# Heads of one layer in two 40-row halves, gate pieces together and one product for both memories in a two-layer memory transformer

## The chip, the cores and the metric

The kernel runs on one core of a Trainium2 chip. The metric is the device time of one execution in microseconds (us); lower is better. All times below are us unless marked ns. PE is TensorE, DVE is VectorE, ACT is ScalarE, POOL is GpSimd and SP is SyncE, which issues most transfers.

## The reference

Two layers run one after the other over x of 2048 rows and 448 columns (bf16). Each layer is a recurrent memory attention A and a gated feed-forward part B, both behind a layer norm and with the same weights in both layers:

```python
for s in range(n_seg):                          # 64 segments of 32 rows
    h = concatenate([mem, x[:, 32*s : 32*s+32]])  # 8 memory rows + 32 rows
    q, k, v = h @ Wq, h @ Wk, h @ Wv            # 16 heads of 256
    p = softmax(mask(q @ k.T * 256**-0.5))
    o = (p @ v) @ Wo
    mem = o[:, :8]                              # read by the next segment
    outs.append(o[:, 8:])
# A: x = x + outs;   B: x = x + (relu(n @ W_gate) * (n @ W_up)) @ W_down, n = layernorm(x), 1792 hidden
```

The mask lets every row see the 8 memory rows, and a row of the segment see itself and the rows before it. Since a segment needs the memory of the one before, the 64 segments of a layer are a chain.

## The kernel before

**Folding.** Scores are h M h^T with M = Wk Wq^T for each head, and the output is P h B with B = Wv Wo. M and B (tiles M_sb, MT_sb, B_sb, BT_sb) are made once, while the first steps run. The 448 columns are handled as three slices of 128 and a tail of 64; the tail products use half the PE array (64 rows), in pairs.

**Steps.** There are 70 steps, g = 0 to 69. Layer 1 is chain C1, layer 2 is chain C2, which runs 6 steps (LAG) behind. Steps 0 to 5 work on C1 alone and 64 to 69 on C2 alone (function single, L599); steps 6 to 63 work on both (function dual, L803). One step does, in PE's order:

1. G = M h for all heads (tile gps in PSUM, copied to G by ACT and DVE; GPhase.run). The first G products of a step read the memory columns of hTr that the step before wrote last.
2. The mask product that begins the scores' tile S_ps, then the hook mid() with other work.
3. The tails of the memory values and of the scores, then the three main slices of the scores.
4. The softmax on DVE and ACT: reduce (mx), subtract (se), exp, sum, reciprocal, weighting into PW, and a transpose of P in 32x32 blocks on DVE into TW.
5. Beside it, on PE, the values h B (tile vps): VOm of the memory rows and of half a segment, vox of a segment. Class Values does this in parts; ACT and DVE copy each bank (L419). The hooks soft(), before() and late() put other work between them.
6. The output product: AT_ps (rows) or, in steps of one layer that do not end a block, yt and yt3 (function columns, L760, transposed already).
7. The memory rows are turned into columns (mps) and copied into hTr for the next step; the hooks end() and last() follow.

The order of PE's instructions is the order in which the code records them (in_order); DVE, ACT and POOL are ordered by the tile scheduler. PSUM is one pool of eight banks.

**In a step of one layer** the scores stand in two tiles SX and SM of 160 columns, four groups of 32 rows each, the tails wait once on POOL for a token (pass_on, fence), and TW comes from two DVE transposes (L665).

**The feed-forward part** works on blocks of 128 rows, when four segments of a chain are done. It is cut into ten pieces: turn, seven gate_up of 28 products each (PSUM tiles gate and up, copied by ACT to ut and by DVE to hh), and two downs of seven products each (dps; the second adds into x_ring at L358). They wait in ffn_q, one queue for each chain, and fill(chain, n) takes n of them. Which hook takes how many depends on g % 4. Steps with g % 4 == 1 read:

```python
def mid():
    prep_rows(C1, gb + 2, recent["G"])
    fill(0, 2)                      # two gate_up
def before():
    fill(0, 3)                      # one gate_up, two downs
    prep_stats(C2, gb - 1)
    prep_rows(C2, gb - 1)
```

prep_stats and prep_rows make the normalized rows (xn) of the next block: statistics on DVE (L258, L260), the power on POOL (L262, L263), the scaling on DVE (L276). prep_pe in end() turns xn on PE (tps) and copies it to hTr (L298). In single, load_when ties a load of feed-forward weights on SP's queue to certain instructions.

Of the kernel before, what the change touches and what calls it, by code (L numbers as in the profile page):

```python
# [9 lines left out]
BF = mybir.dt.bfloat16  # L10
# [25 lines left out]
RB2 = 64  # L36
NR = 12
# [13 lines left out]
def build_kernel(ctx, tc, A_x, A_mem0, A_Wq, A_Wk, A_Wv, A_Wo, B_W_gate, B_W_up, B_W_down, out,  # L51
# [18 lines left out]
    make_identity(nc, ident[:])  # L70

# [60 lines left out]
    def matmul(*a, **k):  # L132
        op = nc.tensor.matmul(*a, **k)  # L133
        in_order(op)
        if fence:
            sync(op, fence.pop())
# [15 lines left out]
    for q in PWs + [TW]:  # L152
        nc.gpsimd.memset(q[:], 0.0)
# [445 lines left out]
    def single(g, c, inG, mid, soft, before, late, end, last):  # L599
# [7 lines left out]
        mT = memTp[g % 2]  # L607
        SX, SM = [psum.tile([P, 512], F32, tag="ps", name="S_ps") for _ in HALVES]
        N = 4 * L
        matmul(SX[:, 0:N], selq[LO], maskb[LO, 0:4], start=True, stop=False, skip_group_check=True)  # L610
# [3 lines left out]
        vm = Values(lambda rr, k: mT[rr, k, :], VOm, [cp_a, cp_a, cp_a, cp_a])  # L614
        cols = hT[:, :, cid, 0:SEG], mT

        def tails(m, k, e):
            half = HALVES[e]
            ps = (SX, SM)[m][32 * k:32 * k + 32, 0:N].rearrange("p (s e t) -> p s e t", s=2, e=2)
            matmul(ps[:, :, e, :], cols[m][half, 3, :], G[half, :, 7 * k + 3, cid, :], start=(m == 1 and e == 1),  # L620
                   stop=False, tile_position=(half.start, 32 * k), skip_group_check=True)

        for e in range(2):
            for k in range(4):
                tails(0, k, e)
                tails(1, k, 1 - e)
            if not e:
                passed = pass_on()
                if g:
                    vm.both(True)  # L630
                fence.append(passed)
        for m, ps in enumerate((SX, SM)):
            for sl in range(3):
                for k in range(4):
                    t = 7 * k + sl
                    matmul(ps[32 * k:32 * k + 32, 0:N], cols[m][:, sl, :], G[:, :, t:t + 5:4, cid, :], start=False,
                           stop=(sl == 2), tile_position=(0, 32 * k), skip_group_check=True)

        mx = p_soft.tile([P, H], F32, tag="mx", name="mx")
# [3 lines left out]
        for m, ps in enumerate((SX, SM)):  # L643
            q = slice(4 * m, 4 * m + 4)
            S3 = ps[:, 0:N].rearrange("p (h k) -> p h k", k=L)
            nc.vector.tensor_reduce(mx[:, q], S3, axis=AX.X, op=ALU.max)
            nc.vector.tensor_tensor(se[:, q], S3, mx[:, q].unsqueeze(2).to_broadcast([P, 4, L]), op=ALU.subtract)
            vm.after = nc.scalar.activation(se[:, q], se[:, q], AF.Exp, scale=SCALE)
            load_when(vm.after)
        nc.vector.tensor_reduce(ssum[:, 0:8], se[:, 0:8], axis=AX.X, op=ALU.add)  # L650
        nc.vector.reciprocal(rs[:, 0:8], ssum[:, 0:8])
        PW = PWs[g % 2]
        odd = g % 2

        def weigh(kind, slots, keys):

            dst = PW[:, 8 * kind:8 * kind + 8].rearrange("p (g m) t -> p m g t", m=2)
            n = keys.stop - keys.start
            nc.vector.tensor_tensor(dst[:, :, :, slots], se[:, 0:8, keys].rearrange("p (m g) t -> p m g t", m=2),
                                    rs[:, 0:8].rearrange("p (m g) -> p m g", m=2).unsqueeze(3).to_broadcast([P, 2, 4, n]),  # L660
                                    op=ALU.mult)

        def turn_P(kind):
            b = slice(8 * kind, 8 * kind + 8)
            load_when(nc.vector.transpose(TW[:, b, :].rearrange("p b t -> p (b t)"),  # L665
                                          PW[:, b, :].rearrange("p b t -> p (b t)")))

        if odd:
            weigh(1, slice(0, 16 + MEM), slice(16, L))
            turn_P(1)  # L670
            weigh(0, slice(0, 16), slice(0, 16))
        else:
            weigh(1, slice(16, 16 + MEM), slice(SEG, L))
            turn_P(1)
            weigh(0, slice(0, SEG), slice(0, SEG))
        turn_P(0)
# [26 lines left out]
        if v is not None:  # L703
            v.bank(1 - odd, 0)
            v.bank(1 - odd, 1)
        late()

        flat = TW[:, :, :].rearrange("p b t -> p (b t)")
        order = [(1, 0), (1, 1), (1, 2), (1, 3), (0, 0), (0, 1), (0, 2), (0, 3)]
        nxt = g + 1 - c.lag < nseg  # L710
        if nxt and not ends:
            columns(g, c, flat, (vox, VOm), order)
            end()
            last()
            return
        at = [psum.tile([P, 512], F32, tag="ps", name="AT_ps") for _ in HALVES]
        cols = (slice(0, 256), slice(256, DM))
        for kind, gs in order:
            src = (vox, VOm)[kind]
            side, e = divmod(gs, 2)  # L720
            o = 64 * (4 * kind + gs)
            for half, ps, cc in zip(HALVES, at, cols):
                matmul(ps[half, 0:cc.stop - cc.start], flat[:, o:o + 64], src[:, 2 * e + side, cc],
                       start=((kind, gs) == order[0]), stop=((kind, gs) == order[-1]), tile_position=(0, half.start),
                       skip_group_check=True)
# [7 lines left out]
        if nxt:  # L733
            tps = [psum.tile([P, 2, MEM], F32, tag="ps", name="mps") for _ in HALVES]
            m = slice(SEG, L)
            for kd in range(2):
                for half, ps in zip(HALVES, tps):
                    for lo in ((0,) if kd == 0 or half is LO else (0, 64)):
                        w = mb[half, 128 * kd:128 * kd + (64 if kd and half is HI else 128)]
                        o = ps[lo:lo + 64, kd] if kd and half is HI else ps[:, kd]  # L740
                        matmul(o, w, ident[half, half.start + SEG + 16:half.start + L + 16], start=True, stop=True,
                               skip_group_check=True)
            r = (g + 1) % NR
            cp_v(hTr[:, r, 0:2, cid, SEG:L], tps[0][:])
            op = cp_a(hTr[:, r, 2:4, cid, SEG:L], tps[1][:])
            if ut is not None:
                behind(ut, op)
            columns_of(g + 1, [c])
# [11 lines left out]
    def columns(g, c, flat, src, order):  # L760

        yt, yt3 = [psum.tile([P, 512], F32, tag="ps", name=n) for n in ("yt", "yt3")]
        W = L + 16

        def mains(some):
            for kind, gs in some:
                side, e = divmod(gs, 2)
                o = 64 * (4 * kind + gs)
                for sl in range(3):
                    matmul(yt[:, sl * W:sl * W + W], src[kind][:, 2 * e + side, 128 * sl:128 * sl + 128],  # L770
                           flat[:, o:o + W], start=((kind, gs) == order[0] and not sl),
                           stop=((kind, gs) == order[-1]), skip_group_check=True)

        mains(order[:6])
        for kind, gs in order:
            side, e = divmod(gs, 2)
            o = 64 * (4 * kind + gs)
            for half in HALVES:
                matmul(yt3[half, 0:W], src[kind][:, 2 * e + side, 384:DM], flat[:, o:o + W],
                       start=((kind, gs) == order[0]), stop=((kind, gs) == order[-1]), tile_position=(0, half.start),  # L780
                       skip_group_check=True)
        mains(order[6:])
        hT = hTr[:, (g + 1) % NR, :, c.cid]
        ym = yt[:, 0:3 * W].rearrange("p (k t) -> p k t", t=W)
        cp_v(hT[:, 3, SEG:L], yt3[:, W - MEM:W])
        cp_v(hT[:, 0:3, SEG:L], ym[:, :, W - MEM:W])
# [16 lines left out]
    def dual(g, chains, inG, mid, soft, before, late, end, last):  # L803
# [141 lines left out]
        if nxt:  # L945
            tps = {c.cid: psum.tile([P, NSL, MEM], F32, tag="ps", name="mps") for c in nxt}
            for kd in (2, 3, 1, 0):
                for c in nxt:
                    half = HALVES[c.cid]
                    m = c.rb + SEG  # L950
                    matmul(tps[c.cid][:, kd], mb[half, 128 * kd:128 * kd + 128], ident[half, m:m + MEM],
                           start=True, stop=True, skip_group_check=True)
            for c in nxt:
                eng = cp_v if c is C1 and not ends else cp_a
                op = eng(hTr[:, (g + 1) % NR, :, c.cid, SEG:L], tps[c.cid][:])
                if ut is not None and eng == cp_a:
                    behind(ut, op)
            columns_of(g + 1, nxt)
# [66 lines left out]
    for g in range(nsteps):  # L1025
# [25 lines left out]
        elif r == 1:  # L1051
# [3 lines left out]
            def mid():  # L1055
                prep_rows(C1, gb + 2, recent["G"])
                fill(0, 2)

            def before():
                fill(0, 3)  # L1060
                prep_stats(C2, gb - 1)
                prep_rows(C2, gb - 1)

# [98 lines left out]
```

## Time and profile before

| what | value |
|---|---|
| median of 9 runs | 1517.39 us |
| lowest and highest | 1514.95 and 1519.29 us |
| profiled execution: its time | 1515.34 us |
| profiled execution: span | 1513.5 us |
| PE busy, share of the span | 1484.7 us, 98% |
| DVE, ACT, POOL busy | 958.9, 600.8, 150.5 us |
| steps of both layers, by g % 4 = 0, 1, 2, 3 | 21.75, 24.32, 20.95, 19.25 us |
| steps 0 to 5 | 35.42, 13.59, 13.04, 14.48, 15.04, 18.55 us |
| steps 64 to 69 | 16.56, 20.45, 15.73, 15.36, 12.23, 27.53 us |

The length of a step is taken from its first G product to that of the next step. Step 0's length holds the start of the kernel's main part, and step 69's the last feed-forward block. In the lines of a timeline the columns are start, length, engine, line, operation, output<-input, tile size, shape and count. A product's "length" in such a line includes a pipeline of some 150 to 250 ns, so the distance of starts, not the length, is what it costs PE. In the chain the columns are start, length, what. In the list of waits they are what waited, for whom, in total, how often and the longest.

### The profile page before, as it was taken

What the parts mean: (1) busy time and instruction counts of PE and PEld (TensorE: products, weight loads), DVE (VectorE), ACT (ScalarE), POOL (GpSimd) and SP (SyncE); (2) the same over time, 40 slices, a digit from 0 to 9 for tenths busy, and PEclk for the clock granted to TensorE, in tenths of its full rate; (3) what the DMA queues carried; (4) which work ended last, traced back from release to release, by engine and by line L of the source; (5) the groups of instructions that cost most, each with busy time, mean ns of one, the idle gap of its engine ahead of it and who ended that gap; (6) DMA issues with size and microseconds to landing.
All of it is one profiled execution on the core that took longest, in us unless ns stands there. A gap on an engine that the chain in (4) does not pass through costs nothing.

```text
span 1513.5 us, 89312 instructions
## 1 busy us (share of the span) xinstructions
PE 1484.7 (98%) x41984; PEld 1139.6 (75%) x41984; DVE 958.9 (63%) x2236; ACT 600.8 (40%) x1410; POOL 150.5 (10%) x534
## 2 busy tenths in 40 slices
PE   7999999999999999999999999999999999999998
PEld 4567777778777777877778777877778777877786
DVE  6635566666666566666666666666666665666544
ACT  5644333433344343434343343434334343434343
POOL 1001011010101001010100101010001100011000
PEclk9999999999999999999999999999999999999999
DMA  9731001010000100010000000000000000000000
GB/s 234 175 95 41 5 13 15 12 20 13 14 14 15 18 12 20 12 22 13 8 19 14 20 12 20 12 21 7 15 18 13 17 12 15 13 6 14 5 8 9
DMA packets 82801, 39.40 MB, mean 26 GB/s; under 512 B 65176, under 2 KB 81536, under 8 KB 82432
## 3 DMA queue, kind: packets, MB, share of 16 engines
q1 hardware_dynamic: 82400, 33.68, 10.1%
q8 instruction: 328, 5.37, 1.4%
q14 instruction: 41, 0.34, 0.1%
q10 hardware_dynamic: 32, 0.01, 0.0%
HBM read 14.00 MB, written 1.84 MB: 10 GB/s over the span
## 4 chain that ended last, share of the span: by engine, by line
PE 95%; DMA 2%; DVE 2%; SPq 1%; ACT 1%; issue 1%; POOL 0%; POOLq 0%; ACTq 0%
PE gps L133 31%; PE vps L133 29%; PE gate L133 9%; PE S_ps L133 6%; PE AT_ps L133 6%; PE dps L133 6%; PE up L133 3%; PE ps L133 2%; DMA xnT<-xd 1%; PE yt L133 1%; SPq L175 1%; PE mps L133 0%; DMA wq<-in_A_Wq_dram 0%; PE tp L145 0%; DMA wvn<-in_A_Wv_dram 0%
## 5 line engine op out<-in xcount | busy, mean ns | idle before, releaser
L133 PE MATMUL gps<-hTr,M_sb 128*128 128x80 bf16 (+1 forms) x11760 | 413.6, 198 | 2.4 <-issue 2.4
L133 PEld LDWEIGHTS <-M_sb 128*128 128x128 bf16 x11760 | 403.9, 99 | 7.0 <-issue 2.8
L495 DVE CAST G<-gps 128x480 bf16<-128x480 f32 (+4 forms) x327 | 194.7, 611 | 217.4 <-PE gps L133 217.0
L495 ACT CAST G<-gps 128x480 bf16<-128x480 f32 (+4 forms) x327 | 165.6, 525 | 340.4 <-PE gps L133 340.4
L133 PEld LDWEIGHTS <-hTr 128*32 128x32 bf16 (+1 forms) x8512 | 174.7, 95 | 161.4 <-issue 44.9
L133 PE MATMUL vps<-B_sb,hTr 128*32 128x448 bf16 x4464 | 234.2, 353 | 0.0
L133 PE MATMUL gate<-xnT,Wgu 64*128 64x128 bf16 x3136 | 204.5, 217 | 1.8 <-ACT xnT L333 1.0
L133 PE MATMUL up<-xnT,Wgu 64*128 64x128 bf16 x3136 | 204.7, 217 | 0.5 <-issue 0.5
L133 PEld LDWEIGHTS <-Wgu 64*128 64x128 bf16 x6272 | 186.0, 94 | 21.3 <-issue 19.3
L133 PEld LDWEIGHTS <-memTp 128*32 128x32 bf16 (+1 forms) x5880 | 136.9, 95 | 64.8 <-issue 2.4
L133 PE MATMUL vps<-B_sb,memTp 128*32 128x448 bf16 x3360 | 171.7, 353 | 0.2 <-issue 0.2
L419 ACT CAST vox<-vps 128x448 bf16<-128x448 f32 x186 | 96.1, 533 | 186.2 <-PE vps L133 186.2
L346 DVE SCALAR_TENSOR_TENSOR hh<-gate,ut 128x256 bf16<-128x256 f32 x224 | 93.6, 418 | 66.5 <-ACT ut L345 66.3
L419 ACT CAST VOm<-vps 128x448 bf16<-128x448 f32 x251 | 120.7, 526 | 1.5 <-PE vps L133 1.4
L345 ACT CAST ut<-up 128x256 bf16<-128x256 f32 x224 | 83.8, 374 | 73.1 <-PE up L133 72.4
L419 DVE CAST vox<-vps 128x448 bf16<-128x448 f32 x186 | 104.7, 599 | 5.6 <-PE vps L133 5.4
L133 PEld LDWEIGHTS <-TW 128*32 128x32 bf16 (+1 forms) x3760 | 93.1, 97 | 13.4 <-DVE TW L665 1.9
L862 ACT ACTIVATE se<-se 128x320 f32<-128x320 f32 x116 | 54.5, 470 | 117.2 <-DVE se L861 117.2
L133 PE MATMUL gps<-hTr,MT_sb 64*128 64x80 bf16 (+1 forms) x3920 | 91.5, 195 | 2.9 <-ACT MT_sb L197 0.7
L133 PE MATMUL dps<-Wd,hh 128*128 128x448 bf16 x448 | 92.7, 354 | 0.0
L892 DVE STREAM_TRANSPOSE TW<-PW 128x512 bf16<-128x512 bf16 x116 | 75.3, 685 | 21.1 <-POOL PW L874 21.1
L133 PEld LDWEIGHTS <-MT_sb 64*128 64x128 bf16 x3920 | 76.3, 96 | 14.1 <-DVE mv L260 4.8
(110 smaller groups left out, 1411.4 us busy)
## 6 DMA issues: line engine op xcount, KB each, us to landing
wo<-in_A_Wo_dram SPq DMA_DIRECT2D x8, 448.0 KB, 5.6
wvn<-in_A_Wv_dram SPq DMA_DIRECT2D x8, 384.0 KB, 3.9
y<-mb SPq DMA_DIRECT2D x87, 28.0 KB, 1.8
out_dram<-x_ring SPq DMA_DIRECT2D x16, 112.0 KB, 1.7
Wgu<-in_B_W_gate_dram SPq DMA_DIRECT2D x7, 224.0 KB, 3.3
Wgu<-in_B_W_up_dram SPq DMA_DIRECT2D x7, 224.0 KB, 3.3
Wd<-in_B_W_down_dram SPq DMA_DIRECT2D x7, 224.0 KB, 2.7
x_ring<-in_A_x_dram SPq DMA_DIRECT2D x10, 112.0 KB, 2.9
```

Source lines behind the costliest of these rows:

```text
L133: op = nc.tensor.matmul(*a, **k)
L175: in_order(nc.sync.dma_start_transpose(t[:], srcs[n][:, 1024 * i:1024 * (i + 1)]))
L345: recent["ut"] = nc.scalar.copy(ut[:], gu[1][:])
L346: recent["hh"] = nc.vector.scalar_tensor_tensor(out=self.hh[:, f:f + 2, :], in0=gu[0][:], scalar=0.0, in1=ut[:], op0=ALU.max, op1=ALU.mult)
L419: op = self.evac[2 * x + e](self.dst[:, 2 * e + x, :], self.ps[x][e][:, 0:DM])
L495: op = (cp_a, cp_v)[self.side](gp.G[:, self.side, self.t0:self.t0 + self.n, gp.c0:gp.c1, :], self.ps[:, 0:self.n * gp.NP].rearrange("p (m ...
L862: vm.after = nc.scalar.activation(se[:, q], se[:, q], AF.Exp, scale=SCALE)
L892: load_when(nc.vector.transpose(TW[:, b, :].rearrange("p b t -> p (b t)"), PW[:, b, :].rearrange("p b t -> p (b t)")))
```

## The change

The change has four parts.

- In single, the scores of a step stand in one tile of 320 columns: eight heads in rows 0 to 39, eight in rows 64 to 103 (sel, PARTS). The token on POOL goes. The softmax runs once over 104 rows. P is transposed by four PE transposes into PT_ps, two copied by ACT, two by DVE, between the two value banks. Columns are 40 wide in place of 56.
- In steps with g % 4 == 1, mid() takes three gate_up and before() the two downs.
- In step 5 (g + 1 == LAG), what was before() becomes soft(), so the downs and the statistics and rows of C2 come ahead of the memory values' mains.
- In dual, with g % 4 == 1 and both chains going on, the two memories are turned by four products over 128 rows and one ACT copy, in place of eight over 64 rows and two copies.

```diff
+PARTS = (slice(0, SEG), slice(SEG, L))
+    sel = glob.tile([P, P], BF)
+    for half in HALVES:
+        nc.vector.tensor_tensor(sel[:, half], ident[:, LO], ident[:, HI], op=ALU.add)
...
+    PT = p_pp.tile([P, 4, P], BF, name="PT")
...
     def single(...)
-        SX, SM = [psum.tile([P, 512], F32, tag="ps", name="S_ps") for _ in HALVES]
-        N = 4 * L
-        matmul(SX[:, 0:N], selq[LO], maskb[LO, 0:4], start=True, stop=False, skip_group_check=True)
+        S = psum.tile([P, 512], F32, tag="ps", name="S_ps")
+        N = 8 * L
+        matmul(S[:, 0:N], sel[LO, :], maskb[LO], start=True, stop=False, skip_group_check=True)
         mid()
...
-        for e in range(2):
-            for k in range(4):
-                tails(0, k, e)
-                tails(1, k, 1 - e)
-            if not e:
-                passed = pass_on()
-                if g:
-                    vm.both(True)
-                fence.append(passed)
...
+        def S_tail(e, stop):
+            half = HALVES[e]
+            for q in PARTS:
+                r = 64 * e + q.start
+                matmul(S[r:r + q.stop - q.start, 0:N], hT[half, 3, cid, q], G[half, :, 3:NGH:7, cid, :], start=False,
+                       stop=stop, tile_position=(half.start, r), skip_group_check=True)
+
+        if g:
+            for e in range(2):
+                vm.part(e, True)
+                S_tail(e, False)
...
+        for sl in range(3):
+            for e in range(2):
+                for q in PARTS:
+                    r = 64 * e + q.start
+                    matmul(S[r:r + q.stop - q.start, 0:N], hT[:, sl, cid, q], G[:, :, sl + 4 * e:sl + 4 * e + 22:7, cid, :],
+                           start=False, stop=(g > 0 and sl == 2), tile_position=(0, r), skip_group_check=True)
...
+        nc.vector.tensor_reduce(mx[R2, 0], S3, axis=AX.X, op=ALU.max)
+        nc.vector.tensor_tensor(se[R2, 0:8], S3, mx[R2, 0].unsqueeze(2).to_broadcast([n, 8, L]), op=ALU.subtract)
+        vm.after = nc.scalar.activation(se[R2, 0:8], se[R2, 0:8], AF.Exp, scale=SCALE)
...
-        def turn_P(kind):
-            b = slice(8 * kind, 8 * kind + 8)
-            load_when(nc.vector.transpose(TW[:, b, :].rearrange("p b t -> p (b t)"),
-                                          PW[:, b, :].rearrange("p b t -> p (b t)")))
...
         before()
         if v is not None:
             v.bank(1 - odd, 0)
+        for q, Pt, cp in ((0, Px, cp_a), (2, Pm, cp_v)):
+            PT_ps = psum.tile([P, 4, P], BF, tag="ps", name="PT_ps")
+            for x in range(2):
+                transpose(PT_ps[:, x, R2], Pt[R2, 4 * x:4 * x + 4, :], ident[R2, R2])
+            load_when(cp(PT[:, q:q + 2, R2], PT_ps[:, 0:2, R2]))
+        late()
+        if v is not None:
             v.bank(1 - odd, 1)
-        late()
...
     def dual(...)
         if nxt:
...
+            if len(nxt) == 2 and g % 4 == 1:
+                tps = psum.tile([P, NSL, 2, MEM], F32, tag="ps", name="mps")
+                pick = ident[:, :].rearrange("p (c t) -> p c t", c=2)[:, :, SEG:L]
+                for kd in (2, 3, 1, 0):
+                    matmul(tps[:, kd], mb[:, 128 * kd:128 * kd + 128], pick, start=True, stop=True,
+                           skip_group_check=True)
+                cp_a(hTr[:, (g + 1) % NR, :, :, SEG:L], tps[:])
+            else:
...
         elif r == 1:
             def mid():
                 prep_rows(C1, gb + 2, recent["G"])
+                fill(0, 3)
+
+            def before():
                 fill(0, 2)
-
-            def before():
-                fill(0, 3)
                 prep_stats(C2, gb - 1)
                 prep_rows(C2, gb - 1)
+
+            if g + 1 == LAG:
+                soft, before = before, none
```

## The prediction

> **What bounds the kernel now.** I read the page first (busy shares, then the chain that ended last), then PE's list of waits, then single stretches as timelines and chains: one dual step with g % 4 == 1 (step 21, 474.67 to 498.99), one step of C2 alone (66), the last step of C1 alone (5) and an early one (2).
>
> ```profile
> span 1513.5 us, 89312 instructions
> PE 1484.7 (98%) x41984; PEld 1139.6 (75%) x41984; DVE 958.9 (63%) x2236; ACT 600.8 (40%) x1410; POOL 150.5 (10%) x534
> PE 95%; DMA 2%; DVE 2%; SPq 1%; ACT 1%; issue 1%; POOL 0%; POOLq 0%; ACTq 0%
> ```
>
> PE is the chain (95%), at a granted clock of 0.999. So time can be won or lost in two ways only: PE's own starts (how many products, how far apart, how many changes of array shape), and the rare waits of PE. Those waits are few:
>
> ```profile
> PE tps L145 <- DVE xn L276: 3.0, 3, 1.7
> PE gps L133 <- issue: 2.4, 4, 1.2
> PE AT_ps L133 <- DVE TW L665: 1.1, 1, 1.1
> PE S_ps L133 <- POOL token L140: 0.2, 1, 0.2
> ```
>
> The profiled run took 1515.34 with a span of 1513.5; the median of the nine runs, 1517.39, is 2.05 above it. I sum differences against the profiled run and put them on the median. 0.2% is 3.0 us, about what a measurement of this kernel can tell from no change.
>
> **Part 1: dual steps with g % 4 == 1 and both memories going on (9, 13, ... 61: 14 of them).** Step lengths from first G product to first G product: 24.32 for nearly all. The timeline of step 21, PE's rows:
>
> ```profile
> 488.78 0.57 PE L133 MATMUL vps<-BT_sb,hTr 64*32 64x448 bf16 x16
> ...
> 490.18 2.82 PE L133 MATMUL dps<-Wd,hh 128*128 128x448 bf16 x14
> ...
> 497.05 0.39 PE L145 MATMUL tps<-ident,xn 128*128 128x128 bf16 x4
> 497.37 0.26 PE L133 MATMUL mps<-ident,mb 64*128 64x8 bf16 x8
> 497.55 1.50 PE L133 MATMUL dps<-Wd,hh 128*128 128x448 bf16 x7
> ```
>
> Between the value tails (64x32 tiles) and the downs lies the third gate piece, 28 products of 64x128. From the last tail's start, 489.009 in the single records, to the first down is 1.169. Without the piece one change of shape remains: tail to another shape takes 0.281. In mid() the piece follows two others of the same shape, which run at 27.75 ns a start (56 in 1.79 with one change): 28 x 27.75 = 0.777. So 1.169 - 0.281 - 0.777 = 0.111 saved per step, which is one drain: in the same records the change from tails to gate costs 281 where 187 is usual, and gate to downs 148 where 56 is.
>
> The memories' turn: from the last tps start (497.216) to the next down (497.554) is 0.338, of which 0.151 is the change to 64x128, then eight products at about 24 ns. After: no change of shape, 56 ns for the last tps, then four 128x128 loads with 16 columns. The trace has none of 16 columns; the nearest row is G's 128x128 products with 40 columns, 25 to 28 ns a start. 56 + 4 x 27 = 0.164, so 0.174 saved. Bounds: if starts were only as dense as the transposes (56 ns) 0.06 would be saved; at 24 ns a start 0.186.
>
> Sum 0.285 x 14 = **-4.0** (bounds -2.4 to -4.3). What has to hide: the third hh is done before the softmax's first reduce; the transposed P comes 0.78 later, near 491.6, against AT's start at 494; the third hh, which the downs read, comes before them and not beside them. One ACT copy instead of two lies under the 1.43 of the last downs. The tight cover is DVE's:
>
> ```profile
> 497.76 0.63 DVE L258 BATCH_NORM_STATS2 stats<-x_ring 128x6 f32<-128x448 bf16 x1
> 498.42 0.29 DVE L298 COPY hTr<-tps 128x256 bf16<-128x256 bf16 x1
> ```
>
> C2's new columns are in hTr at 498.71; the next G starts at 498.99. After, DVE's chain hangs on AT, which moves by 0.111 (to 498.60), and G moves by 0.285 (to 498.70). The margin is 0.1; if it is gone, up to 0.1 to 0.18 a step is lost.
>
> **Part 2: the 12 steps of one layer (0 to 5, 64 to 69).** S becomes one tile of 320 columns in two 40-row halves. Its mask product streams 320 columns, not 160: +0.07. Mains: 12 products of 320 in groups of four, instead of 24 of 160: 0.54 against 0.47, which is in the yt times below. The tails no longer need POOL's token, and need fewer G copies at once. Early steps waited there; the chain in step 2:
>
> ```profile
> 69.66 0.21 PE S_ps L133 x8
> ...
> 69.92 0.11 POOL token L140
> ...
> 70.07 0.58 PE S_ps L133 x20
> ```
>
> Tails and mains took 1.24, 1.17 and 1.02 in steps 1 to 3 and 0.90 in 68, against 0.70 where nothing waits: I take 0.33, 0.45, 0.33 and 0.2 off, -1.3 in all.
>
> Against that stand four transposes on PE in place of two on DVE. In step 66 the old ones cost PE nothing:
>
> ```profile
> 1449.89 0.76 DVE L665 STREAM_TRANSPOSE TW<-PW 128x256 bf16<-128x256 bf16 x2
> ...
> 1451.02 1.32 PE L133 MATMUL vps<-B_sb,hTr 128*32 128x448 bf16 x24
> ...
> 1452.27 0.48 PE L133 MATMUL yt<-TW,VOm 128*128 128x56 bf16 x12
> ```
>
> TW is whole at 1450.65, while PE wants it at 1452.27. The four transposes go between the two value banks: one change of shape in (0.105), three starts at 56 (0.168), one out (0.151): 0.42, whether or not anything waits. S mains start at 1446.41. The new softmax (one reduce 0.49, one subtract 0.49, exp 0.47, sum 0.48, reciprocal 0.2, two weighings 0.5) is ready some 3.6 after the first S main; PE comes at 3.8. The copies are new waits: DVE's copy of P's transpose stands behind its vox copy (0.6), and with it yt starts 4.83 after the first S main instead of 4.36. I take 0.47 a step (bounds 0.22, four starts of 56 ns, and 1.0, if exp queues behind a VOm copy of 0.51 on ACT). Steps 0 to 4, 64 and 66 to 68: 9 x 0.47 = +4.2, nine mask products +0.6, waits -1.3: **+3.5**. Narrower columns (40, not 56) save nothing: both start every 27 ns. In 69 PE waited 1.1 for TW, and the new path through PE and a copy is about as long: 0. In 65 a chain of x_ring, statistics, rstd, xn sets the end as before: 0. load_when's weights move one issue later on SP's queue, long before their use: 0. Setup: two DVE adds and a POOL memset while PE waits for the first weights: 0.
>
> The Trainium skill speaks against this part: "TensorE: Matmul & The Clock Gate", Part 4: PE-mode transpose, gives about 275 ns to a transpose in a kernel and asks for a copy out of PSUM. By that figure four would be an estimated 1.1 us, and the twelve steps about 9 us dearer than my sum. This trace's transposes last 219 ns each but start every 56 ns, so I hold to the starts; the copy is in the sum.
>
> **Part 3: step 5.** Its downs now run ahead of the memory values' mains. Before:
>
> ```profile
> 152.78 0.64 DVE x_ring L358
> ...
> 155.28 0.41 DVE xn L276
> ...
> 155.74 0.46 PE tps L145 x4
> ...
> 156.56 0.96 PE gps L133 x37
> ```
>
> PE stood 1.9 before the second tps. Downs that end near 150.3 put this chain's end near 153.4. But DVE's order has P's transposed copy behind xn: it comes at 153.45, yt starts at 153.75 and not 153.1, and takes 1.1; tps follow at 154.85, and the two hTr copies let G start at about 156.05: **-0.5** (0 if DVE is later still; -1.9 if the copy does not hold yt).
>
> **Pauses of PE that nothing explains.** The 2.4 under issue and some smaller gaps lie a multiple of 128 products apart in the steps of one layer, some 0.5 each, 5 us in all; the regular spacing suggests the loading of instructions, which the page lists as a queue of its own, but no row proves it. About 300 products fewer is two such places fewer of some 28: -0.3 (bounds -1.5 and +1, since all places shift).
>
> **Sum:** -4.0 + 3.5 - 0.5 - 0.3 = **-1.3**: 1514.0 for the profiled run, 1516.1 on the median. Its own range, 1514.2 to 1518.1.
>
> **Rivals.**
> *A, the steps of one layer cost less.* The old steps also change shape before yt, so the transposes may cost only their four starts (0.22): -2.2 in nine steps; step 5 gets its whole 1.9: -1.4. For it: DVE and ACT are less busy in these steps. Against: DVE's order in step 5. All of it is -4.9; with most of it -4.5, 1512.9.
> *B, slower: P's transpose becomes a wait.* Place: the copy of P's transpose on DVE in the nine steps. The softmax now starts only when all of S is done, exp stands behind the first VOm copy on ACT's queue, and with the PE margin of 0.2 gone, the second value bank is late as well. Price 1.0 instead of 0.47: -1.3 + 9 x 0.53 = +3.5, 1520.9. It decides from 0.95 a step. For it: the thin margin. Against: in step 66 that VOm copy (1447.88, 0.51) would end 1.9 after the first S main, so exp, wanted at 1.7, is held by 0.2 alone.
> *C, the saving of part 1 does not reach the next G*, since DVE's copy of hTr ends last: 14 x 0.18 given back, +1.2, 1518.6.
>
> **How the numbers follow.** My sum 0.40 (0.06 of it beyond -3.0), A 0.36, B 0.17, C 0.07. Faster: 0.36 + 0.06 = 0.42; within: 0.34 + 0.07 = 0.41; slower: 0.17. The range runs from past A's -4.9 to most of B, 1511.8 to 1520.5: about 1 in 10 is left out on each side.
>
> **What would show it.** Steps 9 to 61 with g % 4 == 1 at 24.03 instead of 24.32, gate pieces in one run, four mps of 128x16. Steps 64, 66 and 67 longer by about 0.5, with PT_ps near 3.8 after S. Step 5 at about 18.0. The other dual steps unchanged at 21.75, 20.95 and 19.25. I am wrong if PE waits for PT in the steps of one layer by over 0.3, if hTr releases G after the steps of part 1, or if steps that the diff does not touch change.

## The result and the profile after

The changed kernel takes 1510.16 us (median of 10 runs, 1508.47 to 1512.63) beside 1517.12 of the kernel before (32 runs, 1513.36 to 1521.28). The ratio is 0.9954 with a 95% interval of 0.9944 to 0.9963: 7.0 us faster. The forecast was -1.3, and the time lies below its range, 1511.8 to 1520.5. Its profiled run took 1511.46, of which the span is 1509.7.

The page of the changed kernel, the lines that answer to those of before:

```profile
span 1509.7 us, 88653 instructions
PE 1484.4 (98%) x41688; PEld 1136.0 (75%) x41688; DVE 953.2 (63%) x2202; ACT 603.0 (40%) x1396; POOL 149.9 (10%) x523
PE 95%; DMA 1%; DVE 1%; SPq 1%; ACT 1%; issue 0%; POOL 0%; POOLq 0%; ACTq 0%
```

PE is still the chain, and its busy time is the same within 0.3 us: this sum can't show where 7 us went. PE's list of waits:

```profile
PE gps L138 <- issue: 1.7, 4, 0.7
PE yt L138 <- DVE PT L701: 1.2, 1, 1.2
PE AT_ps L138 <- DVE PT L701: 1.1, 2, 0.7
PE tps L150 <- DVE xn L282: 0.6, 1, 0.6
```

The tps waits for xn fell from 3.0 to 0.6, and waits for P's transposed copy (PT) came in their place, in steps 5, 65 and 69. The wait for POOL's token is gone.

**Dual steps.** All 14 with g % 4 == 1 take 0.30 less (most of them 24.32 before and 24.02 after, forecast 24.03); the other dual steps stand at 21.75, 20.95 and 19.25 as before, save for step 6 and for single excursions of up to 0.7 in both profiles. Step 21's PE rows after:

```profile
489.12 0.57 PE L138 MATMUL vps<-BT_sb,hTr 64*32 64x448 bf16 x16
489.62 2.82 PE L138 MATMUL dps<-Wd,hh 128*128 128x448 bf16 x14
...
496.50 0.39 PE L150 MATMUL tps<-ident,xn 128*128 128x128 bf16 x4
496.72 0.25 PE L138 MATMUL mps<-ident,mb 128*128 128x16 bf16 x4
496.82 1.49 PE L138 MATMUL dps<-Wd,hh 128*128 128x448 bf16 x7
```

The downs follow the value tails after 0.50 and not 1.40, since the third gate piece now stands in mid(), and from tps to the next downs it is 0.32, not 0.50. The four products over 128 rows start about 25 ns apart. 14 x 0.30 = 4.2 of the 7.0 are here.

**Steps of one layer.** From the profile before to the one after, steps 0 to 5 become 2.1 shorter in all, step 6 becomes 1.5 longer, steps 64 to 68 become 2.2 longer and step 69 becomes 2.3 shorter. Two things that have nothing to do with the amount of work make up much of these differences: falls of PE's granted clock, and pauses of PE, in which it stands and no row names what it waits for. The clock first. Rows of the view by stretches (length, busy time and count of PE, PEld, DVE, ACT, POOL, then the granted clock, DMA share and GB/s) in the last feed-forward block, before:

```profile
1500.13:1502.00 1.87, 1.87 (x40) 1.87 (x41) 0.00 (x0) 0.35 (x1) 0.00 (x0) 0.57 0.18 58
1502.00:1504.00 2.00, 2.00 (x47) 2.00 (x43) 0.85 (x2) 0.40 (x2) 0.00 (x0) 0.55 0.00 0
1504.00:1507.30 3.30, 3.30 (x122) 3.23 (x116) 1.51 (x4) 1.49 (x4) 0.00 (x0) 1.00 0.02 5
```

and of the changed kernel, the same block and then the beginning of step 6:

```profile
1497.95:1500.00 2.05, 2.05 (x74) 2.05 (x75) 0.42 (x1) 0.64 (x2) 0.00 (x0) 1.00 0.13 45
...
155.98:157.30 1.32, 1.32 (x37) 1.21 (x36) 0.00 (x0) 0.46 (x2) 0.00 (x0) 0.50 0.00 0
157.30:159.00 1.70, 1.70 (x28) 1.70 (x27) 0.00 (x0) 0.29 (x1) 0.00 (x0) 0.50 0.00 0
```

For 3.4 us the clock is half, the same products start every 53 ns and not every 28, and 1.7 us are lost. PE is "busy" all the while, so no busy sum shows it. Each profile has such falls at other places: that of before has one, the block above; that of the changed kernel has two, in the setup (at 33) and in step 6. In the profiles of all the kernels below, 23 falls lie ahead of the program's last product. Each lasts 3.41 us, falls of one run lie a whole multiple of 3.41 us apart (30.0, 36.0, 13.0 and so on), and in the 3.41 us ahead of each PE had stood for 1.3 to 2.3 in all. Stretches of this grid with up to 1.9 of standing had no fall behind them, so the standing time alone does not tell when a fall comes. The mean clock of a run tells how many falls it had. Over 34 runs of the kernel before, beside the first experiments:

| mean clock | runs | mean time |
|---|---|---|
| 1.000 | 2 | 1514.0 |
| 0.999 | 10 | 1515.8 |
| 0.998 | 16 | 1517.3 |
| 0.997 | 6 | 1519.9 |

Their mean is 0.9982; the changed kernel's is 0.9991, and 0.0009 of 1513 us is 1.3 to 1.4 us. (The kernel before had 0.9984 to 0.9987 in the later groups of runs.)

### The profile page after: what moved, and what is told of

It is laid out like the page before. It is cut to its first block, busy times and chain, and to the rows that moved or that the text cites. A ratio compares the mean times of both kernels' runs of the same rounds, so it can differ in the third digit from the quotient of the medians.

```text
span 1509.7 us, 88653 instructions
## 1 busy us (share of the span) xinstructions
PE 1484.4 (98%) x41688; PEld 1136.0 (75%) x41688; DVE 953.2 (63%) x2202; ACT 603.0 (40%) x1396; POOL 149.9 (10%) x523
## 4 chain that ended last, share of the span: by engine, by line
PE 95%; DMA 1%; DVE 1%; SPq 1%; ACT 1%; issue 0%; POOL 0%; POOLq 0%; ACTq 0%
PE gps L138 32%; PE vps L138 29%; PE gate L138 8%; PE AT_ps L138 6%; PE S_ps L138 6%; PE dps L138 5%; PE up L138 4%; PE ps L138 2%; PE yt L138 1%; DMA xnT<-xd 1%; SPq L181 1%; PE mps L138 0%; DMA wq<-in_A_Wq_dram 0%; PE tp L150 0%; DMA wvn<-in_A_Wv_dram 0%
## 5 line engine op out<-in xcount | busy, mean ns | idle before, releaser
L138 PEld LDWEIGHTS <-hTr 128*32 128x32 bf16 (+2 forms) x8464 | 172.4, 95 | 160.2 <-issue 47.6
L138 PE MATMUL gate<-xnT,Wgu 64*128 64x128 bf16 x3136 | 199.8, 216 | 1.4 <-ACT xnT L339 1.0
L138 PE MATMUL up<-xnT,Wgu 64*128 64x128 bf16 x3136 | 200.0, 216 | 0.0
L138 PEld LDWEIGHTS <-memTp 128*32 128x32 bf16 (+1 forms) x5640 | 131.4, 95 | 66.5 <-issue 2.3
L138 PEld LDWEIGHTS <-TW 128*32 128x32 bf16 x3712 | 90.8, 97 | 11.0 <-DVE TW L885 0.7
```

## The experiments

Theory 1 says that products and waits of PE alone set the time, theory 2 that falls of PE's clock after gaps do as well, theory 3 that pauses of PE that come with its number of instructions do. Medians stand beside the runs of the kernel before in the same group of runs (1517.1, 1517.5, 1516.5, 1517.0 and 1516.7).

**1. The kernel before once more** (no edit).

> The kernel before, unchanged, to see its spread and where PE's granted clock falls. Theory 1 (products and waits alone): the ratio is 1, and the runs differ by some 0.5 us around their median, with no pattern in the clock. Theory 2 (clock): PE's granted clock falls to 0.5 for some 3.4 us after stretches in which PE idles, each fall costs about 1.6 us and lowers a run's mean clock by 0.001; so the runs spread over some 5 us, the profile shows one to three falls, and these lie behind the second tps of step 5, the tps waits of steps 65 and 69 or the setup, not always the same. Theory 3 (pauses of PE without a releaser): they stay where they were, at the same products, and are about 5 us again.

1517.61, ratio 1.0003 (0.9993 to 1.0013), mean clock 0.9982. The profile has a fall in step 0 and one in step 6, none in the last block (step 69: 25.62, not 27.53). In step 6, after the 1.89 wait of step 5:

```profile
159.77:161.50 1.73, 1.73 (x57) 1.66 (x57) 0.00 (x0) 0.35 (x1) 0.00 (x0) 0.85 0.03 9
161.50:164.50 3.00, 3.00 (x50) 3.00 (x48) 0.66 (x1) 1.07 (x2) 0.00 (x0) 0.52 0.00 0
```

The places differ from run to run, as theory 2 has it.

**2. The dual part alone.**

```diff
 mid():    fill(0, 2) -> fill(0, 3)      before(): fill(0, 3) -> fill(0, 2)
 dual:     four 128x128 mps products, one ACT copy, for g % 4 == 1
```

> Only the three gate pieces in mid() for g % 4 == 1 and the one product for both memories; heads and step 5 as before. Theory 1: the 14 dual steps with g % 4 == 1 at 24.02 (-0.30 each, -4.2), step 65 0 to -1 by its earlier downs; -4.2 to -5.2 in all, so 1512 to 1513 beside 1517.1. Theory 2: about the same -4.2, and -1 to -2 more if the tps wait of step 65 was a place of clock falls. If the whole gain of 7.0 is here, the heads and step 5 are worth nothing.

1513.29, ratio 0.9975 (0.9966 to 0.9985): -3.8. The 14 steps are at 24.02. Mean clock 0.9983, as before.

**3. The gate pieces alone** (one run).

> The kernel before with three gate pieces in mid() and two downs in before() for g % 4 == 1, and nothing else. Prediction: 24.32 - 0.11 = 24.21 in the 14 dual steps; with the changed kernel's 24.02 the memories' one product then has 0.19 (predicted 0.17). Step 65 shorter by 0.3 to 0.6, since its downs end earlier and its tps no longer wait.

The one run took 1515.13, which alone says nothing. The steps with g % 4 == 1 are at 24.21, to the hundredth what was forecast, so the memories' product has 0.19. Step 65 took 20.22 (20.45 before), less than expected. The profile of step 21:

```profile
492.55 0.57 PE L133 MATMUL vps<-BT_sb,hTr 64*32 64x448 bf16 x16
493.06 2.82 PE L133 MATMUL dps<-Wd,hh 128*128 128x448 bf16 x14
...
500.25 0.26 PE L133 MATMUL mps<-ident,mb 64*128 64x8 bf16 x8
500.43 1.50 PE L133 MATMUL dps<-Wd,hh 128*128 128x448 bf16 x7
```

**4. The heads alone** (single, columns, sel and PT of the changed kernel).

> Only the heads of one layer in two 40-row halves (with the PE transposes, the 40-wide columns, the new setup tiles); steps with g % 4 == 1 and step 5 as before. My prediction: +3.5 -0.3, so about +3.2. Theory 1 with the sizes of the changed kernel's profile: +0.4 in each of steps 4, 64, 66, 67 and about -0.5 in steps 1 to 3, -0.7 in 69: 0 to -1. Theory 2: a further -1 to -2 from fewer falls of the clock. Theory 3: the pauses move to other products, +1 to -2.

1514.81, ratio 0.9985 (0.9977 to 0.9994): -2.3. My +3.2 looked plainly wrong here; experiments 12 to 17 say more.

**5. The swap in step 5 alone.**

```diff
+            if g + 1 == LAG:
+                soft, before = before, none
```

> Only the downs, statistics and rows of step 5 ahead of the memory values' mains (the hooks swapped at g + 1 == LAG). Prediction: without the PE transposes nothing holds yt, so the second tps no longer waits 1.9: -1.0 to -1.9. Theory 1: just that. Theory 2: up to -1.6 more where the clock fell after that wait, in the share of runs in which it did: -2 to -3 in the median.

1515.41, ratio 0.9988 (0.9980 to 0.9997): -1.7. The second tps waits no more, but the downs now wait 0.6 for the last hh, so step 5 itself went from 18.34 (18.55 in the first profile) to 18.14 only. The mean clock rose from 0.9982 to 0.9992, some 1.4 of the 1.7. Most of the gain is the clock.

**6. Useless work in the gaps of the kernel before.**

```diff
+    def warm(n):
+        ps = psum.tile([P, 4, P], BF, tag="ps", name="warm_ps")
+        for i in range(n):
+            transpose(ps[:, i % 4], ident[:], ident[:])
 end():  prep_pe(C1, gb + 2); fill(1, 1)
+        warm(31) in step 5, warm(19) in step 65
         prep_pe(C2, gb - 1)
 turn(): + warm(20) ahead of and warm(20) behind the tps of step 69
```

> The kernel before with useless PE transposes of the identity put into four of its gaps: 31 ahead of the second tps of step 5 (a wait of 1.89), 19 ahead of the tps of step 65 (1.11), 20 ahead of the tps of step 69 and 20 behind them (1.2 each). Theory 1 (only products and waits count): the gaps are filled, nothing becomes faster, 0 to +0.5. Theory 2 (clock): the granted clock no longer falls in step 6 or in the last feed-forward block; the mean clock rises from 0.9982 to about 0.9992, and the median falls by 1.0 to 2.0 although PE has 90 products more.

1514.29, ratio 0.9981 (0.9972 to 0.9989): 90 products more and 3.2 us less. The mean clock is 0.9995, the profile has no fall at all before the end. Theory 1 falls. The gain is more than expected: the kernel before stood at 0.9985 in this group, so the clock accounts for some 1.4 of it, and the rest is open.

**7. Useless work in step 5 alone** (the 31 of experiment 6).

> The kernel before with the 31 useless transposes ahead of the second tps of step 5 alone. If the 1.89 wait of step 5 is the main place of clock falls, as step 5's swap alone (mean clock 0.99917) suggests: mean clock near 0.9990, median -1.2 to -2. If the gaps of steps 65 and 69 are: mean clock stays at 0.9982 to 0.9985, median 0 to -0.5. Theory 1: 0.

1514.33, ratio 0.9983 (0.9973 to 0.9993), mean clock 0.9993. This is 2.2 less, so most of experiment 6's 3.2 comes from step 5. The beginning of step 6 stands at full clock; the one fall is in the last block, where the gaps were left. Two stretches around the beginning of step 6:

```profile
156.00:160.00 4.00, 3.61 (x112) 3.37 (x111) 0.96 (x3) 1.35 (x3) 0.00 (x0) 1.00 0.02 4
160.00:163.00 3.00, 3.00 (x90) 3.00 (x86) 1.31 (x2) 0.70 (x2) 0.00 (x0) 1.00 0.00 0
```

**8. The changed kernel with its gaps filled** (warm(22) and warm(14) ahead of yt and AT in steps 5 and 65, four fillings in step 69).

> The changed kernel with useless PE transposes in the gaps that it still has: 22 between P's transposes and yt in step 5, 14 there in step 65, 14 ahead of and 8 behind P's transposes in step 69, 20 ahead of and 20 behind the tps of step 69. Theory 2 (clock): the mean clock rises from 0.9991 to 0.9996 or more, no fall in step 6 or in the last feed-forward block, and the median falls by 0.5 to 1.3 to about 1509. Theory 1: 0 to +0.5.

1509.50 (6 runs), ratio 0.9944 (0.9931 to 0.9956), mean clock 0.9993 beside 0.9991. The direction is right, but the interval overlaps the changed kernel's: inconclusive.

**9. PT's second copy on ACT in steps 5 and 65.**

```diff
-        for q, Pt, cp in ((0, Px, cp_a), (2, Pm, cp_v)):
+        for q, Pt, cp in ((0, Px, cp_a), (2, Pm, cp_a if g in (LAG - 1, nseg + 1) else cp_v)):
```

> The changed kernel with the second copy of P's transpose on ACT, not DVE, in steps 5 and 65 only. If DVE's queue is what holds yt in step 5 (PE waits 1.36 there) and AT in step 65 (0.91): those waits go; step 5 falls from 18.4 to about 17.5 to 17.9, step 65 by 0 to 0.9 (its tps may wait for the same chain instead); -1.0 to -1.8 in all, with the fall of the clock in step 6 rarer. If it is the softmax that is late: no change.

1510.88 (5 runs), ratio 0.9967 (0.9955 to 0.9980): no gain. In step 5 the wait for PT fell from 1.2 to 0.8, and from P's first transpose to yt it was 1.18 and not 1.51, so DVE's queue held yt by some 0.3. But the step didn't shorten (18.48; 18.37 in the changed kernel), since pauses in the scores ahead of it took 0.4 more in this profile. In step 65 nothing changed (19.91 and 19.95).

**10. P's transposes twice.**

```diff
-            for x in range(2):
+            for x in (0, 1, 0, 1):
                 transpose(PT_ps[:, x, R2], ...)
```

> The changed kernel with each of the four transposes of P done twice, so that its time tells what four PE transposes cost. My prediction (four starts of 56 ns on PE's path): +0.22 to +0.25 in ten steps (in 5 and 69 part of it lies in a wait), +2.2 to +2.5. If a transpose costs its duration of 0.2 or more: +0.8 a step, +8. If they lie in a wait: 0.

1510.25 (5 runs), ratio 0.9956 (0.9944 to 0.9968). The medians can't tell 0 from +1.5, but the steps without pauses can: step 4 goes from 15.46 to 15.64 and step 64 from 16.89 to 17.02. Four transposes cost 0.13 to 0.18, 33 to 45 ns each (in the trace they start 46 ns apart), not their duration.

**11. POOL's token in the changed kernel.**

```diff
                 S_tail(e, False)
+                if not e:
+                    fence.append(pass_on())
```

> The changed kernel with POOL's token put back between the two halves of the scores' tails in steps 1 to 5 and 64 to 69, as in the kernel before. If the token is what the tails waited for in the steps without feed-forward work: +0.2 to +0.3 in each of steps 1, 2, 3, 68 and 69 and up to 0.2 in the others, +1 to +2.5. If they waited for the copies of G: 0 to +0.5.

1517.59, ratio 1.0001 (0.9991 to 1.0010): +7.4, far above the forecast. From the first tail to the end of the scores' mains each of the 11 steps is longer by 0.53 to 0.61, 6.4 in all. The timeline of step 4:

```profile
129.79 0.30 PE L138 MATMUL S_ps<-G,hTr 64*32 64x320 bf16 x2
130.16 0.10 POOL L145 MEMSET token<- 128x1 f32 x1 [5.65 <-PE S_ps L138]
...
130.31 0.38 PE L138 MATMUL vps<-BT_sb,memTp 64*32 64x448 bf16 x8 [0.22 <-POOL token L145]
```

From PE's product to POOL and back it is 0.52. Here the very next product waits; in the kernel before 16 tails of the memory values lay between, and hid most of it (1.07 for tails and mains in step 4, 1.05 in the changed kernel). So this run shows the price of a token without cover, not what the old heads paid.

**12. 64 useless products ahead of everything, in the changed kernel.**

```diff
+    warm(64)
     make_two(0)
```

> The changed kernel with 64 useless PE transposes in front of everything, where PE waits for its first weights. If the unexplained pauses of PE come with the number of instructions (every 128 products with their 128 weight loads): they move by 64 products, from place 90 of 128 in steps 1 to 5 to place 26, and from 78 to 14 in steps 64 to 69; the time changes by -1 to +1.5, since other work stands there. If they come from the work itself: they stay in the G products where they are, and the time is the same.

1513.65, ratio 0.9976 (0.9965 to 0.9986): 3.4 slower than the changed kernel. Counted from the program's first product, the pauses are still at place 90 of every 128 in steps 1 to 5 and at 78 in steps 64 to 69, so in the work they moved by 64 products. (The kernels with the old heads have them at 90 and at 74 to 76.) Theory 3 holds: they come with the number of instructions. They hit steps 2 and 3 harder there (14.23 and 14.94, not 12.48 and 13.47), and the mean clock fell to 0.9982. The longest one in the first profile of before, and the page's rows of the instruction queue before and after (packets, MB, share):

```profile
112.20 0.97 PE L133 MATMUL gps<-hTr,M_sb 128*128 128x40 bf16 x32 [1.20 <-issue]
```

```profile
q8 instruction: 328, 5.37, 1.4%
```

```profile
q8 instruction: 326, 5.34, 1.4%
```

2 x 41984 products and weight loads over 328 packets is 256 a packet; 2 x 41688 over 256 is 325.7. One packet for 128 products fits the spacing of the pauses. Their times fit too. Ahead of the pause above the queue's one packet ran from 109.59 to 110.70; the same view from 109.55 to 110.75 has it:

```profile
q8 instruction: 1, 0.02, 5.8%
```

PE went on at 112.20, 1.50 after its end. In all the profiles together, PE's gaps of 0.1 or more without a releaser, from step 1 on, are 108. Every one of them lies in a step of one layer and ends 1.2 to 1.7 after the end of a packet of this queue, where one product in ten of these steps would by chance. So the pauses hang on the loading of instructions; no row names the releaser, and why a packet comes late is not shown.

**13. The same in the kernel before.**

> The kernel before with 64 useless PE transposes ahead of everything. If the placing of the pauses is chance, the kernel before moves too, by -2 to +3.5 against itself, as the changed kernel did (+3.4). If the kernel before already lies badly: 0 or below.

1512.69, ratio 0.9977 (0.9967 to 0.9987): 4.3 faster, by work that does nothing. Steps 1 to 3 took 12.59, 12.45 and 13.49 (13.59, 13.04 and 14.48 before), with 0.8 of pauses in their G products in place of 2.9 (what the starts lie apart beyond 28 ns).

**14. The heads alone with the 64 products.**

> Heads in two halves alone, with the same 64 transposes. If the heads' gain of 2.3 is their own work: 2 to 2.5 below before_shift64. If it is the placing of pauses and clock falls: within 1 of before_shift64 or above it, and far from 1514.8.

1517.48, ratio 1.0007 (0.9998 to 1.0017): 4.8 slower than experiment 13. The heads that gained 2.3 in one placing lose 4.8 in the other.

**15. The change without the heads** (dual part and swap).

> The changed kernel with the heads of the kernel before (dual part and step 5's swap alone). By sums of the single runs, -3.8 and -1.7: -5.5, about 1511.6, and the heads are worth 1.4 inside the change. If the heads' own work costs what their steps show without pauses (about 0): within 1 of 1510.2. If my forecast of +3.5 for them were right: 1506.7.

1510.40 (8 runs), ratio 0.9960 (0.9947 to 0.9973). In the change itself the heads are worth 0.2, which is nothing. Step 5 took 17.27 here, so the swap shortens it by over 1 when P's transposes don't come between.

**16. The changed kernel with 32 products ahead.**

> The changed kernel with 32 useless transposes ahead of everything. If placing decides: anywhere from -1 to +3.5 against 1510.2, with the pauses at places 90 and 78 of 128 as counted from the first product. If 64 transposes cost by their own time in the setup: half of the 3.4, +1.7.

1509.92 (6 runs), ratio 0.9955 (0.9940 to 0.9971): unchanged. Nothing here shows a price of the idle products themselves, of their time or of the turn of a PSUM bank that they take. The interval alone doesn't exclude half of 3.4, but the same 64 made the kernel before faster (experiment 13).

**17 and 18. Dual part, swap and old heads with 64 products ahead; the same with step 69's gaps filled.**

> Dual part, step 5's swap, old heads, and the 64 transposes at the start. If placing works as in the kernel before (-4.3): 1506 to 1507. If the placing is good by chance for one kernel only: 1509 to 1514.

> The same with 20 useless transposes ahead of and 20 behind the tps of step 69. Theory 2 (clock): no fall in the last block; the mean clock is higher by about 0.0003 and the median lower by 0.3 to 0.7 than no_heads_shift64. Theory 1: the same or +0.2.

1506.21 (5 runs), ratio 0.9929 (0.9916 to 0.9943), and 1507.06 (5 runs), ratio 0.9937 (0.9924 to 0.9949). The first is the fastest kernel of all, 4 us below the changed one; the placing adds to the other parts. Filling step 69 has shown nothing: the intervals overlap.

## Why the prediction was wrong

**Dual part: right.** Forecast -0.111 and -0.174 a step, measured -0.11 and -0.19; -4.0 became -4.2 in the steps and -3.8 in the medians (experiment 2). (The outer bound adds up to -4.2, 14 x 0.297, not to -4.3.) DVE's tight cover of 0.1 held: after 13 of the 14 steps the next G waits for nothing, and after step 9 it waits 0.30 for hTr, where it stood 0.36 before as well. Rival C is out.

**Step 5: the order right, the second price missing.** The chain ran in the forecast's order: PT's copy behind xn, then yt, tps and G. Counted from the step's first G product yt came 0.6 later than forecast and the next G 0.3 later: the step took 18.37 (about 18.0 forecast, 18.55 before). The chain of step 5 after:

```profile
153.52 0.18 DVE xn L287
153.70 0.18 DVE PT L701
...
153.92 1.22 PE yt L138 x40
155.14 0.24 PE tps L150 x4
...
155.98 0.55 PE gps L138 x11
```

But the term was -0.5, and beside the dual part and the old heads the swap is worth 2.9 (experiment 2 against 15: 1513.3 to 1510.4; by the two ratios 2.3). The step itself has over 1 of it there, but beside the new heads it gains only 0.4 (18.80 in the profile of experiment 4). The mean clock's rise, 0.9983 to 0.9989, is 0.9 at most, for the kernel before stood higher by 0.0004 in the second group as well; the rest is open. I had counted the 1.9 wait of step 5 as time lost once; its second price, a half clock in step 6 in some of the runs, stood in no row of the one profile that I had, because the fall of that run lay in the last block. There it could be seen: 196 gate products in 7.21, 37 ns each, where 28 is usual. I didn't look at the clock by stretches, since the page's line reads 9 in all 40 slices: a slice is 38 us, and 3.4 us at half clock leave it above 0.95.

The Trainium skill bears on this, "TensorE: Matmul & The Clock Gate", What's actually happening: the gate halves PE's clock after an idle window of about 3.4 us, the window runs free of the program, and the other state comes back after a window of work. The length (3.41), the factor (0.50) and the free window (falls whole multiples of 3.41 apart) agree here. The idle window doesn't: PE had stood for only 1.3 to 2.3 of the 3.41 us ahead of each fall, in one wait or in several. Two of the falls followed pauses (1.38 in step 2 of experiment 15, 1.48 in step 3 of experiment 3), so pauses can cost the clock too.

**Heads: the price of the transposes nearly right, the sum overturned by placing.** From the first S main to yt, steps 2 to 4 went from 4.36 to 4.76, +0.40 where I took 0.47 (the mains took 0.42 before and after, and not 0.47 and 0.54). My 4.36 was theirs; in step 66, whose lines I showed, it was 5.86. Step 66 after:

```profile
1448.31 0.36 PE L150 MATMUL PT_ps<-ident,PW 104*128 104x104 bf16 x4
1448.67 0.33 ACT L701 COPY PT<-PT_ps 128x208 bf16<-128x208 bf16 x1 [0.53 <-PE PT_ps L150]
1448.97 0.26 DVE L701 COPY PT<-PT_ps 128x208 bf16<-128x208 bf16 x1
1449.29 0.47 PE L138 MATMUL yt<-PT,VOm 128*128 128x40 bf16 x12
```

The copy ends at 1449.23, ahead of yt at 1449.29: the margin is under 0.1, and it held; rival B, which spoke of nine such steps, is out. Where I had put 0, PE does wait for PT: 1.2 in step 5, 0.7 in step 65 and 0.4 in step 69, over the 0.3 that I had named as a sign of being wrong. The waits were under-sized: I took off 1.3, while tails and mains take 1.05 in all 11 steps after (1.16 in step 5) and took 1.06 to 2.12 before, 3.3 less in all (the mean of two profiles). That is more than the token: part of it is pauses, for in step 2 the same stretch took 1.58, 2.12 and 1.33 in three profiles of the old heads, and 1.05 and 2.08 with the new. Step 65 was forecast at 0 and gained 0.5. It was no chain of xn alone: the tps waits of 0.76 and 0.26 are gone with the new heads (19.66 in experiment 4), while the gate pieces alone kept them (20.22).

**What failed.** Two terms failed: the -0.5 for step 5, which left out the clock, and the one on pauses, "-0.3 (bounds -1.5 and +1, since all places shift)". The swap came to -2.9 (-2.3 by the ratios), and heads and pauses, +3.2 in my sum, came to -0.2. The change removes 20 products in each of 12 steps, and so moves every later pause. The heads were worth -2.3, +4.8, -0.2 and +7.4 in four pairs (experiments 4; 13 to 14; 15 to the changed kernel; 17 to 12). Their mean is +2.4, not far from my +3.2; the spread is what I had bounded at 1.5. The pair that the change itself makes, -0.2, lies below that mean.

The traces bear out that placing hides the price. Of the steps 1 to 4, 64 and 66 to 68 take the shortest that any profile with the old and with the new heads has: they sum to 2.3 more with the new, beside +3.0 for these eight in my sum. And in the profiles of the four pairs the spans differ by +0.2, +4.5, -0.3 and +10.2; with 1.7 taken off for each fall, and PE's gaps without a releaser taken off (as far as the starts lie apart beyond 28 ns), by +3.2, +1.6, +3.2 and +4.9. These are single profiles, so this is an estimate.

**Together.** In medians, each part beside those before it: -3.8 for the dual part, -2.9 for the swap with its clock, -0.2 for the heads as they lie, -6.9 beside -7.0. In another order swap and heads would share differently (the heads alone gave -2.3). Rival A named heads that cost less and a fuller gain in step 5, and came nearest with 1512.9, but by luck: its transposes cost 0.40 and not 0.22, and step 5 did not get its 1.9. What stays open: why the long pauses appear in the steps of one layer alone, and how long each becomes. G's products start 25 to 28 ns apart there and 36 ns in the dual steps, which leaves a packet more time, but no run tests that.

## What to carry to other kernels

A gap of PE may be paid twice: look at the granted clock in stretches of 1 to 2 us behind every gap, not in 40 slices, and compare the mean clock of the runs before you explain a difference of 0.1%. Where an edit changes the number of PE's instructions, try it at two placings (some dozens of idle products at the start) before you believe a gain or a loss of some us. The lengths of undisturbed steps were forecast to hundredths in the dual part and to some 0.1 in the heads; sums over the rest were not.

## What the hardware showed that I had not expected

- Useless products made the kernel before faster: 31 in one gap by 2.2 (1516.5 to 1514.3), 64 at the start by 4.3.
- A fall of PE's clock lasts 3.41 us at 0.50 and costs 1.7; it follows stretches of 3.41 us in which PE stood for 1.3 to 2.3, in some runs and not in others.
- Pauses without a releaser, 0.1 to 1.5 long, stay at fixed places modulo 128 products of the program, whatever work stands there, and end 1.2 to 1.7 after a packet of the instruction queue.
- The way from PE to POOL and back to PE through a memset of one column took 0.52.
